# A new static order, tables partly on ScalarE, and a half-column transform for one batch, in a fused attention and Fourier-mixing kernel

## The chip, the cores and the metric

The kernel runs on one core of one Trainium2 chip. The metric is the device time of one execution in microseconds (us), as the median over several runs. A core has five engines with instruction queues of their own: PE (TensorE, the matrix engine), DVE (VectorE), ACT (ScalarE), POOL (GpSimd) and SP (SyncE, which here only issues DMA transfers). Matmuls write to PSUM, which has eight banks of 128 partitions by 512 fp32 numbers; everything else lies in SBUF.

## The reference

Four inputs r, k, v and w of shape (4 batches, 8 heads, 768 steps, 48) go through a linear attention with a decaying state; its output, 768 rows of 384 numbers per batch, is mixed by the real part of a two-dimensional Fourier transform, added to itself, normalised and passed through a two-layer perceptron.

```python
# attention, per batch and head; state is 48 x 48
for t in range(S):
    cur = outer(u * k[t], v[t])
    y[t] = r[t] @ (state + cur)
    state = w[t][:, None] * state + outer(k[t], v[t])
# x = y with the heads side by side: (4, 768, 384)
X = np.fft.fft(x, axis=1)                  # over the 768 steps
X = np.fft.fft(X, axis=2)                  # over the 384 columns
u  = x + np.real(X)
mu = mean(u, -1); var = mean((u - mu) ** 2, -1)
un = (u - mu) / sqrt(var + 1e-6)
out = u + np.maximum(un @ w_ch1, 0.0) @ w_ch2      # 384 -> 1536 -> 384
```

## The kernel before

**Chunks.** The 768 steps of each batch are cut in six chunks of 128, named (b,c) below. `attention(b, c)` takes the logarithm of w (ACT, into `LB`), sums it along the steps with two matmuls against masks (lines 773 and 777), takes exponentials, scales r and k (`RH`, `KH`), transposes them (matmuls against an identity in the first 18 chunks, a transposing DMA later, line 819), forms the scores (line 843: 48 rows of the array at a time), masks them (line 848), updates the state (lines 866 to 885; the state matmul is line 869) and forms y (lines 896 and 899) into `X`. `fold` adds and subtracts mirrored columns of `X`, so that the transform over columns needs half the work.

**Mix.** `mix(b)` does the transform over the 768 steps (line 968) into `HCS` and, mirrored by the symmetry of the result, `HCR`; then, for each of six row blocks kb, the transform over columns: three matmuls of 384 columns against the tables `DTM` (line 992), which add up in one PSUM bank. VectorE adds x to the bank (line 997) into `UF` and sums the row; ScalarE or VectorE centres it into `UN`; ScalarE sums the squares. `UN` is transposed (matmuls of line 1027 in the first two batches, a transposing DMA per half batch in the last two, line 1033) into `UNT`. Per half batch come the twelve W1 groups of three matmuls (line 1056), the ReLU into `HT` (line 1062 on VectorE, line 1064 on ScalarE), and three W2 blocks, each of three groups of four matmuls (line 1075), followed by the last scaling and addition (line 1081) and the store (line 1085).

**Tables.** The cosines and sines `CS` and `SS` are made on the chip at the start: integer steps and roundings (`TQ`, `TG`, `TF`) and two sine operations on ScalarE, then mirrored copies, then `DTM` by matmuls against the identity `IDW`. The zero paddings of several buffers are filled at the start, too. TensorE begins with sixteen matmuls (line 1098) on a filled piece of the weight buffer `W1`, and 36 filler matmuls (line 1130) stand in its list.

**Order.** Nothing is scheduled at run time. Every operation is a call of `op`, with one or several engines that may execute it and a planned duration for each. `ORDER`, five lists of operation numbers, says which engine executes what, and in which order. `schedule` replays the lists with the planned durations, chooses PSUM banks and adds a few waits between VectorE and POOL; `emit` then writes each engine's list with the semaphore waits that the data need. So a planned duration has no direct effect on the chip; the lists have. SP's list holds the 96 loads (192 KB each, seven buffers per input), the transposing DMAs and the stores; the three weight loads are issued by POOL: two halves of W1 (line 745) and W2 (line 749).

Of the kernel before, what the change touches and what calls it, by code (L numbers as in the profile page):

```python
# [7 lines left out]
ALU = mybir.AluOpType  # L8
# [27 lines left out]

MEANS = (0, 1, 2, 3)
# [29 lines left out]
    "act": (  # L67
# [14 lines left out]
    "dve": (  # L82
# [14 lines left out]
    "pool": (  # L97
# [12 lines left out]
}  # L110


class _Tile:


    __slots__ = ("bank", "ops", "pool", "n_done", "end")
# [1047 lines left out]
```

## Time and profile before

| | |
|---|---|
| median of 3 runs | 182.72 us (182.53 to 183.22) |
| the profiled execution | 184.21 us, of which the span from first to last instruction is 182.4 us |
| granted TensorE clock | 1.000 |
| busy share of the span | PE 97%, DVE 81%, ACT 71%, POOL 56% |
| HBM | 23.59 MB read, 4.72 MB written, 155 GB/s over the span |
| instructions | 4568, of them 1722 matmuls |

The profile shows one execution. For each engine it gives busy time and idle time, and for idle time what ended it. Rows of a group read: line, engine, operation, what it writes and reads, count, then busy time in us and the mean duration of one in ns, then the idle time before. Matmuls overlap, so the mean duration of one is longer than the distance from one to the next.

### The profile page before, as it was taken

Reading aid. Unit: us, or ns where it says so; the run is one execution under the profiler, and the core shown is the slowest. Engines: PE = TensorE matmul, PEld = TensorE weight load, DVE = VectorE, ACT = ScalarE, POOL = GpSimd, SP = SyncE. Lnnn points to the kernel's source line nnn. Section 1 sums busy time; section 2 is a strip of 40 time slices with the busy share of each in tenths; the row PEclk is TensorE's granted clock in tenths of the full one; section 3 lists DMA queues with packets and bytes.
Section 4 is the critical chain, followed back from the end, with each engine's and each line's share of the span. In section 5 each row is a group of like instructions: output and inputs, shape, how many; then the busy total and the mean of one; then the engine's idle time right before and its main releaser. Section 6 shows DMA issues by size and latency. Waiting matters only on the chain.

```text
span 182.4 us, 4568 instructions
## 1 busy us (share of the span) xinstructions
PE 176.8 (97%) x1722; PEld 116.3 (64%) x1722; DVE 148.2 (81%) x341; ACT 130.2 (71%) x340; POOL 101.5 (56%) x120
## 2 busy tenths in 40 slices
PE   7999999999999999999999999999999999999994
PEld 3465676766566666776657666656666676666663
DVE  8779999899899999999888997899979927622343
ACT  2889859597898675799899978888882247478200
POOL 2448789767231498589998968769653440000000
DMA  4999998999999899999999999997550103331214
GB/s 97 203 216 196 208 191 172 185 202 208 152 196 190 162 210 230 226 204 182 202 222 218 219 177 207 220 212 179 103 114 0 47 2 65 73 125 43 86 71 145
DMA packets 116119, 28.99 MB, mean 159 GB/s; under 512 B 111361, under 2 KB 116098, under 8 KB 116098
## 3 DMA queue, kind: packets, MB, share of 16 engines
q1 hardware_dynamic: 114514, 26.36, 70.2%
q0 software_dynamic: 1584, 2.36, 8.0%
q8 instruction: 13, 0.21, 0.5%
q14 instruction: 8, 0.07, 0.1%
HBM read 23.59 MB, written 4.72 MB: 155 GB/s over the span
## 4 chain that ended last, share of the span: by engine, by line
PE 61%; DVE 17%; DMA 9%; SPq 4%; ACT 4%; issue 3%; DVEq 0%
PE bank L1075 18%; PE bank L1056 17%; DMA in_w<-in_w_dram 5%; DMA w<-in_moe_w_ch_dram 4%; DVE ah L848 4%; SPq L609 4%; PE bank L992 3%; PE bank L1130 3%; PE bank L1098 3%; PE bank L968 3%; DVE osb L1081 2%; PE bank L843 2%; DVE rkh L561 2%; PE bank L889 2%; PE bank L899 2%
## 5 line engine op out<-in xcount | busy, mean ns | idle before, releaser
L1075 PE MATMUL bank<-w,ht 128*128 128x384 bf16 (+2 forms) x300 | 53.7, 320 | 0.0
L1056 PE MATMUL bank<-unt,w 128*128 128x384 bf16 x288 | 51.9, 326 | 0.6 <-DMA w<-in_moe_w_ch_dram 0.6
L1064 ACT ACTIVATE ht<-bank 128x384 bf16<-128x384 f32 x72 | 32.6, 496 | 9.3 <-PE bank L1056 8.9
L1056 PEld LDWEIGHTS bank<-unt,w 128*128 128x128 bf16 x288 | 26.9, 98 | 17.5 <-DVE ht L1062 0.8
L1075 PEld LDWEIGHTS bank<-w,ht 128*128 128x128 bf16 x300 | 27.5, 98 | 15.2
L848 DVE TENSOR_TENSOR ah<-bank,msk 128x512 bf16<-128x512 f32 x48 | 31.2, 682 | 2.1 <-PE bank L843 2.0
L561 POOL TENSOR_TENSOR rk<-rk,ub 128x384 f32<-128x384 f32 x21 | 21.6, 1034 | 8.6 <-DVE rk L561 7.0
L561 POOL TENSOR_TENSOR vtd<-in_v,dc 128x384 f32<-128x384 f32 x20 | 16.7, 837 | 11.2 <-DVE dc L800 8.1
L1081 DVE SCALAR_TENSOR_TENSOR osb<-bank,rstd,uf 128x384 f32<-128x384 f32 (+2 forms) x25 | 14.8, 596 | 9.5 <-PE bank L1075 5.9
L1062 DVE TENSOR_SCALAR ht<-bank 128x384 bf16<-128x384 f32 x24 | 13.0, 549 | 6.9 <-PE bank L1056 6.8
L561 POOL TENSOR_TENSOR rk<-in_r,in_k 128x384 f32<-128x384 f32 x17 | 16.9, 999 | 2.9 <-DMA in_r<-in_r_dram 1.4
L997 DVE SCALAR_TENSOR_TENSOR uf<-bank,x 128x384 f32<-128x384 f32 x24 | 12.5, 553 | 4.7 <-PE bank L992 4.6
L561 POOL TENSOR_TENSOR rkh<-in_k,e 128x384 bf16<-128x384 f32 x14 | 14.1, 1009 | 3.6 <-ACT e L792 2.0
L779 ACT ACTIVATE bank<-bank 128x384 f32<-128x384 f32 x24 | 11.5, 484 | 5.8 <-PE bank L773 5.8
L811 DVE TENSOR_TENSOR rkh<-bank,in_r 128x384 bf16<-128x384 f32 x24 | 13.1, 549 | 2.1 <-ACT bank L779 2.0
L575 ACT ACTIVATE xf<-uf,agg 128x384 bf16<-128x384 f32 x24 | 14.7, 614 | 0.0
L561 POOL TENSOR_TENSOR xf<-sd 128x382 bf16<-128x382 f32 (+1 forms) x10 | 10.6, 1062 | 6.5 <-DVE sd L561 3.0
L575 ACT ACTIVATE lb<-in_w 128x384 bf16<-128x384 f32 x24 | 12.4, 519 | 2.1 <-DMA in_w<-in_w_dram 1.8
L575 ACT ACTIVATE un<-uf,agg 128x384 bf16<-128x384 f32 x18 | 10.6, 611 | 4.1 <-DVE uf L997 4.1
L586 ACT ACTIVATE rkt<-bank 128x256 f32<-128x256 f32 x29 | 10.8, 389 | 3.6 <-PE bank L833 2.4
L561 POOL TENSOR_TENSOR sd<-x 128x385 f32<-128x385 f32 x10 | 10.0, 1015 | 5.9 <-DVE x L908 5.4
L792 ACT ACTIVATE e<-bank 128x392 f32<-128x392 f32 (+1 forms) x24 | 11.7, 497 | 2.3 <-DVE bank L877 1.0
(138 smaller groups left out, 358.7 us busy)
## 6 DMA issues: line engine op xcount, KB each, us to landing
in_w<-in_w_dram SPq DMA_DIRECT2D x24, 192.0 KB, 3.8
in_k<-in_k_dram SPq DMA_DIRECT2D x24, 192.0 KB, 3.8
in_r<-in_r_dram SPq DMA_DIRECT2D x24, 192.0 KB, 4.1
in_v<-in_v_dram SPq DMA_DIRECT2D x24, 192.0 KB, 4.0
out_dram<-osb SPq DMA_DIRECT2D x23, 192.0 KB, 2.8
w<-in_moe_w_ch_dram POOLq DMA_DIRECT2D x2, 576.0 KB, 8.1
w<-in_moe_w_ch_dram POOLq DMA_DIRECT2D x1, 1152.0 KB, 10.7
out_dram<-osb SPq DMA_DIRECT2D x1, 128.0 KB, 1.7
```

Of the source, the lines that this page charges most:

```text
L561: return lambda e: e.tensor_tensor(out=o, in0=a, in1=b, op=f)
L575: return lambda e: e.activation(o, a, f, **kw)
L779: op("act", a_ps(DM) + 20, lambda e: e.activation(ps(tce)[:, 0:DM], ps(tce)[:, 0:DM], ACTF.Exp), w=[tce])
L792: op("act", a_ps(ne), lambda e: e.activation(E2[i2][:, 0:ne], ps(tci)[:, 0:ne], ACTF.Exp), r=[tci], w=[("E2", i2)])
L811: op("dve", v_1(DM), lambda e: e.tensor_tensor(out=rh[:, :, 0:D], in0=ps(tce)[:, 0:DM].rearrange("t (h d) -> t h d", d=D), in1=rt[:, :, :] ...
L848: masked[n] = op("dve", v_1(512), lambda e, x=x: e.tensor_tensor(out=ah[:, x:H:2, :], in0=ps(ta[x])[:, :].rearrange("p (h t) -> p h t", t= ...
L997: op("dve", v_1(DM) + 60, lambda e, kb=kb, t=t: e.scalar_tensor_tensor(out=uf[:, kb, :], in0=ps(t)[:, 0:DM], scalar=1.0, in1=xb[:, kb, 0:D ...
L1056: ins = e.matmul(ps(t)[:, 0:384], W1[:, m, 256 * (j // 2) + j % 2:256 * (j // 2) + 256:2], unt[:, :, m, :], start=(m == 0), stop=(m == NM ...
L1062: {"dve": lambda e, j=j, t=t, ht=ht: e.tensor_scalar(out=ht[:, j, :], in0=ps(t)[:, 0:384], scalar1=su, scalar2=0.0, op0=ALU.mult, op1=ALU. ...
L1064: "act": lambda e, j=j, t=t, ht=ht: e.activation(ht[:, j, :], ps(t)[:, 0:384], ACTF.Relu, scale=su)},
L1075: ins = e.matmul(ps(t)[:, 0:hi - lo], ht[:, j, 128 * x:128 * x + 128], W2[:, j, lo:hi], start=(j == 0), stop=(j == NJ - 1))
L1081: op("dve", v_1(hi - lo) + 64, lambda e, kb=kb, t=t, o=o, lo=lo, hi=hi: e.scalar_tensor_tensor(out=o[:, lo:hi], in0=ps(t)[:, 0:hi - lo], s ...
```

## The change

Seven things change together.

1. In the planner a load takes 920 ns for batch 0 and 1030 ns for the others (960 before), an eviction of `HCS` on ScalarE and the folds on POOL are planned longer, and an operation can be marked as a fence behind the one before it on its engine (the two loads of ScalarE's tables of functions are).
2. Two of the three roundings `TQ`, the zero fills and the mirrored copies may now run on ScalarE; the new order puts two roundings and several fills there.
3. The identity `IDW` is made by VectorE in `NIDW` and copied by ScalarE, as pairs of 16-bit numbers.
4. For batch 3 (`HALF_OUT`) the transform over columns is done in half columns: columns k and 384 - k share a part A and differ in the sign of a part B, so A and B are formed for 193 columns each, and A + B and A - B give all 384. Per row block that is four matmuls of 193 columns, a copy of B by ScalarE, an add and a subtract by VectorE, and the addition of x with the row's sum.
5. Four small operations make the tables for this: `CQ` and the products `DTC`, `DTS` (kept where `CN` and `SN` were).
6. All five lists of `ORDER` are new. 37 operations move from ScalarE to VectorE and 35 the other way, 30 from POOL to VectorE and 28 the other way, 4 from ScalarE to POOL and 2 back. There are 24 operations more.
7. The order of loads, stores and weight loads on SP and POOL is new as part of this.

```diff
+HALF_OUT = (3,)
 ORDER = {
-    "pe": ("7 1414 68 1415 1416 ..."),
+    "pe": ("8 1438 1439 1440 1441 72 ..."),
...
+                if o.fence:
+                    o.deps.add(d)
...
-                if o.xfer == 960:
+                if o.xfer in (920, 1030):
...
-               w=[("in", n, i)], sem="in_%s%d" % (n, i), xfer=960)
+               w=[("in", n, i)], sem="in_%s%d" % (n, i), xfer=920 if b == 0 else 1030)
...
-        dset(384, ts(IDW[:, :], CI[:, :], 0.0, None, ALU.is_equal), r=["CI"], w=["IDB"])
+        dset(384, ts(NIDW[:, :], CI[:, :], 0.0, None, ALU.is_equal), r=["CI"], w=["NIDW"])
+        op("act", a_sb(192), lambda e: e.activation(IDW[:, :].bitcast(FP32), NIDW[:, :].bitcast(FP32), ACTF.Copy),
+           r=["NIDW"], w=["IDB"])
...
+    def zero(o, n, d, x, w):
+        src = TC[:, 0:1].unsqueeze(2).to_broadcast([128, o.shape[1], o.shape[2]])
+        op(None, {"dve": d, "pool": x, "act": a_sb(n)},
+           {"dve": fill(o, 0.0), "pool": fill(o, 0.0), "act": act(o, src, ACTF.Copy, scale=0.0)}, r=["TC"], w=w)
...
-            op(None, {"dve": 266, "pool": 520}, ts(TQ[:, q, :], KI[:, :], TN[:, q:q + 1], MAGIC, ALU.mult, ALU.add),
-               port=("dve",), r=["KI", "TN"], w=[("TQ", q)])
+            f = ts(TQ[:, q, :], KI[:, :], TN[:, q:q + 1], MAGIC, ALU.mult, ALU.add)
+            op(None, {"dve": 266, "pool": 520, "act": a_sb(2 * HQ) + 30},
+               {"dve": f, "pool": f, "act": act(TQ[:, q, :], KI[:, :], ACTF.Identity, scale=TN[:, q:q + 1], bias=MGC[:, :])},
+               port=("dve",), r=["KI", "TN", "MGC"], w=[("TQ", q)])
...
+        if b in HALF_OUT[:1]:
+            for z, T in enumerate((DTC, DTS)):
+                op(None, {"act": a_sb(HE), "dve": v_2(HE)},
+                   {"act": lambda e, z=z, T=T: e.activation(T, DTM[:, 1, 0:HE], ACTF.Copy, scale=CQ[:, z:z + 1]),
+                    "dve": ts(T, DTM[:, 1, 0:HE], CQ[:, z:z + 1], None, ALU.mult)}, port=("dve",),
+                   r=["DTM1", "CQ%d" % z], w=["DTH%d" % z, ("CSn", "SSn")[z]])
...
+            if b in HALF_OUT:
+                t = g.tile("f")
+                for j in (0, 2, 1):
+                    def f(e, j=j, kb=kb, t=t):
+                        a = 128 * (kb % NP)
+                        x = (hcs if kb < NP else HCR)[:, j, a:a + 128]
+                        if j != 1:
+                            return e.matmul(ps(t)[:, (HE if j else 0):(2 * HE if j else HE)], x, DTM[:, j, 0:HE], start=(j == 0),
+                                            stop=False, skip_group_check=True)
+                        e.matmul(ps(t)[:, 0:HE], x, DTC, start=False, stop=True, skip_group_check=True)
+                        return e.matmul(ps(t)[:, HE:2 * HE], x, DTS, start=False, stop=True, skip_group_check=True)
+                    op("pe", mm(HE, 2 if j == 1 else 1), f, ...)
...
+                if b in HALF_OUT:
+                    fs = SD[:, kb % 2, 0, 0:HE]
+                    op("act", a_ps(HE), lambda e, t=t, fs=fs: e.activation(fs, ps(t)[:, HE:2 * HE], ACTF.Copy),
+                       r=[t], w=[("SD", kb % 2, 0)])
+                    op("dve", v_1(HE), lambda e, kb=kb, t=t, fs=fs: e.tensor_tensor(
+                        out=uf[:, kb, 0:HE], in0=ps(t)[:, 0:HE], in1=fs, op=ALU.add), ...)
+                    op("dve", v_1(HE), lambda e, kb=kb, t=t, fs=fs: e.tensor_tensor(
+                        out=uf[:, kb, DM - 1:HE - 1:-1], in0=ps(t)[:, 1:HE - 1], in1=fs[:, 1:HE - 1], op=ALU.subtract), ...)
```

More of the change, by code (lines that the diff above doesn't have):

```diff
@@ L184, in op @@
         o.tiled = tiled
+        o.fence = fence
         for x in r:
@@ L218, in schedule @@
                 o.dur, o.fn, o.port = o.alts[e]
+            for d, o in zip(self.order[e], self.order[e][1:]):
+                if o.fence:
+                    o.deps.add(d)
         for o in self.ops:
@@ L509, in bass_rwkv6_finch__then__fnet_fourier_mix_kernel @@
     DTM = sb("dtm", [3, DM], BF16)
+    CQ = sb("cq", [2], FP32)
     IDW = sb("idw", [384], BF16)
@@ L519, in bass_rwkv6_finch__then__fnet_fourier_mix_kernel @@
     BHPI = sb("bhpi", [1], FP32)
+    MGC = sb("mgc", [1], FP32)
     TCI = sb("tci", [1], mybir.dt.int32)
@@ L579, in vec, with vecx @@
         return op(None, {"pool": p_1(n), "dve": v_1(n)}, fn, port=("dve",), **kw)
+    def vecx(n, fn, **kw):
+        return op(None, {"pool": p_1(n) + 80, "dve": v_1(n)}, fn, port=("dve",), **kw)
     def evict(o, i, n, x=1, more=0, **kw):
@@ L590, in dset @@
         return op("dve", v_2(n), fn, port=("dve",), **kw)
+    MAGIC = 12582912.0
     loads, asked = {}, {}
@@ L627, in small_constants @@
         op("dve", 30, fill(BHPI[:, :], PI / 2), w=["BHPI"])
+        op("dve", 30, fill(MGC[:, :], MAGIC), w=["MGC"])
     def masks():
@@ L647, in bonus, with flip @@
         o = evict(lambda: UB[:, :, :].rearrange("p h d -> p (h d)"), lambda: ps(t)[:, 0:DM], DM, r=[t, "LOGEXP"], w=["UB"])
-    def either(d, x, fn, **kw):
-        return op(None, {"pool": x, "dve": d}, fn, port=("dve",), **kw)
+    def flip(o, i, sg, **kw):
+        f = ts(o, i, sg, None, ALU.mult)
+        return op(None, {"pool": 740, "dve": 260, "act": a_sb(3 * HQ)},
+                  {"pool": f, "dve": f, "act": act(o, i, ACTF.Copy, scale=sg)}, port=("dve",), **kw)
+    def zero(o, n, d, x, w):
+        src = TC[:, 0:1].unsqueeze(2).to_broadcast([128, o.shape[1], o.shape[2]])
+        op(None, {"dve": d, "pool": x, "act": a_sb(n)},
+           {"dve": fill(o, 0.0), "pool": fill(o, 0.0), "act": act(o, src, ACTF.Copy, scale=0.0)}, r=["TC"], w=w)
     def fills():
@@ L656, in fills @@
                 if (n, i) != ("LB", 0):
-                    op(None, {"dve": 75, "pool": 150}, fill(T[i][:, :, D:64], 0.0), w=[(n, i)])
+                    zero(T[i][:, :, D:64], H * (64 - D), 75, 150, [(n, i)])
         for i in range(2):
             for lo, hi, n, z in ((0, 64, "XFn", "XFz"), (446, 512, "XFo", "XFz2")):
-                op(None, {"pool": 250, "dve": 180}, fill(XF[i][:, :, lo:hi], 0.0),
-                   w=[(z, i)] + [(n, i, c) for c in range(NC)])
-            op(None, {"pool": 100, "dve": 60}, fill(X[i][:, :, DM:DM + 4], 0.0), w=[("X", i, c) for c in range(NC)])
-    MAGIC = 12582912.0
+                zero(XF[i][:, :, lo:hi], NC * (hi - lo), 180, 250, [(z, i)] + [(n, i, c) for c in range(NC)])
+            zero(X[i][:, :, DM:DM + 4], NC * 4, 60, 100, [("X", i, c) for c in range(NC)])
     def tables():
@@ L718, in tables_end @@
                r=[(n, q) for q in range(NP)], w=[n + "n"])
-        small(150, ts(NIDW[:, :], IDW[:, :], -1.0, None, ALU.mult), r=["IDB"], w=["NIDW"])
+        op(None, {"dve": 160, "act": a_sb(384)}, {"dve": ts(NIDW[:, :], IDW[:, :], -1.0, None, ALU.mult),
+                                                  "act": act(NIDW[:, :], IDW[:, :], ACTF.Copy, scale=-1.0)},
+           port=("dve",), r=["IDB"], w=["NIDW"])
         small(62, ts(CP[:, :], TC[:, 0:1], 62.5, None, ALU.is_gt), r=["TC"], w=["CP0"])
-        small(62, ts(CP[:, :], CP[:, :], 2.0, -1.0, ALU.mult, ALU.add), r=["CP0"], w=["CP"])
+        small(62, ts(CQ[:, 1:2], CP[:, :], -1.0, 1.0, ALU.mult, ALU.add), r=["CP0"], w=["CQ1"])
+        small(62, ts(CQ[:, 0:1], CP[:, :], 1.0, None, ALU.mult), r=["CP0"], w=["CQ0"])
+        small(62, ts(CP[:, :], CP[:, :], 2.0, -1.0, ALU.mult, ALU.add), r=["CP0"], w=["CP", "CP0"])
         moves = ([(True, 0, 0, 128, -64), (True, 1, 0, 128, 64)],
@@ L919, in fold @@
         if b < FOLD:
-            vec(192, tt(xf[:, c, 64:256], xb[:, c, 0:192], xb[:, c, 384:192:-1], ALU.add),
+            vecx(192, tt(xf[:, c, 64:256], xb[:, c, 0:192], xb[:, c, 384:192:-1], ALU.add),
                 r=[("X", i, c)], w=[("XFe", i, c)])
-            vec(191, tt(xf[:, c, 256:447], xb[:, c, 1:192], xb[:, c, 383:192:-1], ALU.subtract),
+            vecx(191, tt(xf[:, c, 256:447], xb[:, c, 1:192], xb[:, c, 383:192:-1], ALU.subtract),
                 r=[("X", i, c)], w=[("XFo", i, c)])
@@ L936, in fold @@
         have = [("SD", z, 0), ("SD", z, 1)]
-        vec(DM, tt(xf[:, p:NC:NP, 64:256], sd[:, :, 0:192], sd[:, :, 384:192:-1], ALU.add),
+        vecx(DM, tt(xf[:, p:NC:NP, 64:256], sd[:, :, 0:192], sd[:, :, 384:192:-1], ALU.add),
             r=have, w=[("XFe", i, p), ("XFe", i, c)])
-        vec(DM, tt(xf[:, p:NC:NP, 256:447], sd[:, :, 1:192], sd[:, :, 383:192:-1], ALU.subtract),
+        vecx(DM, tt(xf[:, p:NC:NP, 256:447], sd[:, :, 1:192], sd[:, :, 383:192:-1], ALU.subtract),
             r=have, w=[("XFo", i, p), ("XFo", i, c)])
@@ L973, in mix @@
             evict(lambda j=j: hcs[:, j, :].rearrange("p (n x) -> p x n", x=2),
-                  lambda t=t: ps(t)[:, 0:2 * HE].rearrange("p (x n) -> p x n", x=2), 2 * HE, r=[t], w=[("HCS", j)], more=85)
+                  lambda t=t: ps(t)[:, 0:2 * HE].rearrange("p (x n) -> p x n", x=2), 2 * HE, r=[t], w=[("HCS", j)], more=125)
             sg = (1.0, CP[:, :], -1.0)[j]
@@ L987, in mix, with f @@
             n = b * NC + kb
-            t = g.tile("f")
-            for j in range(3):
-                def f(e, j=j, kb=kb, t=t):
-                    a = 128 * (kb % NP)
-                    return e.matmul(ps(t)[:, 0:DM], (hcs if kb < NP else HCR)[:, j, a:a + 128], DTM[:, j, :], start=(j == 0), stop=(j == 2))
-                op("pe", mm(DM), f, r=[("HCS" if kb < NP else "HCR", j), "DTM%d" % j], w=[t])
+            if b in HALF_OUT:
[9 more added lines that the diff above has]
+                        return e.matmul(ps(t)[:, HE:2 * HE], x, DTS, start=False, stop=True, skip_group_check=True)
+                    op("pe", mm(HE, 2 if j == 1 else 1), f, r=[("HCS" if kb < NP else "HCR", j), "DTM%d" % j]
+                       + (["DTH0", "DTH1"] if j == 1 else []), w=[t])
+            else:
+                t = g.tile("f")
+                for j in range(3):
+                    def f(e, j=j, kb=kb, t=t):
+                        a = 128 * (kb % NP)
+                        return e.matmul(ps(t)[:, 0:DM], (hcs if kb < NP else HCR)[:, j, a:a + 128], DTM[:, j, :], start=(j == 0), stop=(j == 2))
+                    op("pe", mm(DM), f, r=[("HCS" if kb < NP else "HCR", j), "DTM%d" % j], w=[t])
             iu = (2 * b + kb // 3) % len(UN)
@@ L996, in mix @@
             if b in MEANS:
-                op("dve", v_1(DM) + 60, lambda e, kb=kb, t=t: e.scalar_tensor_tensor(
-                    out=uf[:, kb, :], in0=ps(t)[:, 0:DM], scalar=1.0, in1=xb[:, kb, 0:DM], op0=ALU.mult, op1=ALU.add,
-                    accum_out=agg[:, kb, 0:1]), r=[t, ("X", i, kb)], w=[("UF", i, kb), ("SUM", i, kb)])
+                if b in HALF_OUT:
[3 more added lines that the diff above has]
+                    op("dve", v_1(HE), lambda e, kb=kb, t=t, fs=fs: e.tensor_tensor(
+                        out=uf[:, kb, 0:HE], in0=ps(t)[:, 0:HE], in1=fs, op=ALU.add),
+                       r=[t, ("SD", kb % 2, 0)], w=[("UFa", i, kb), ("UF", i, kb)])
+                    op("dve", v_1(HE), lambda e, kb=kb, t=t, fs=fs: e.tensor_tensor(
+                        out=uf[:, kb, DM - 1:HE - 1:-1], in0=ps(t)[:, 1:HE - 1], in1=fs[:, 1:HE - 1], op=ALU.subtract),
+                       r=[t, ("SD", kb % 2, 0)], w=[("UFb", i, kb), ("UF", i, kb)])
+                op("dve", v_1(DM) + (60 if b in HALF_OUT else 10), lambda e, kb=kb, t=t: e.scalar_tensor_tensor(
+                    out=uf[:, kb, :], in0=uf[:, kb, :] if b in HALF_OUT else ps(t)[:, 0:DM], scalar=1.0, in1=xb[:, kb, 0:DM],
+                    op0=ALU.mult, op1=ALU.add, accum_out=agg[:, kb, 0:1]),
+                    port=("dve",) if b in HALF_OUT else (),
+                    r=[("UFa", i, kb), ("UFb", i, kb), ("X", i, kb)] if b in HALF_OUT else [t, ("X", i, kb)],
+                    w=[("UF", i, kb), ("SUM", i, kb)])
                 op(None, {"act": a_sb(DM) + 95, "dve": v_2(DM) + 60},
```

13 lines of the change are left out of this document (6 added, 7 removed), and 129 rows, old and new, of the table ORDER.

## The prediction

> **What bounds the kernel now.** I read the page's parts 1 and 2 first, then the chain of waits in order of time, then what TensorE waited for.
>
> ```profile
> span 182.4 us, 4568 instructions
> PE 176.8 (97%) x1722; PEld 116.3 (64%) x1722; DVE 148.2 (81%) x341; ACT 130.2 (71%) x340; POOL 101.5 (56%) x120
> ```
>
> A busy PE need not be a PE at its peak, so 97% alone proves little. The chain settles it (start, length, what):
>
> ```profile
> 1.31 5.30 PE bank L1098 x16
> ...
> 146.27 0.84 PE bank L968 x10
> ...
> 152.00 0.97 PE bank L992 x6
> ...
> 153.78 2.60 PE bank L1075 x16
> 156.38 7.80 PE bank L1056 x48
> ...
> 179.92 0.35 DVE osb L1081
> ```
>
> Divide length by count. 7.80/48 is 162.5 ns for 384 columns, in 2.60/16 and 0.97/6 the same; 0.84/10 is 84 ns for 193 columns. From about 152 to 180 us TensorE issues one matmul after the other at the rate of its columns; the last VectorE piece only closes the chain. The sixteen opening matmuls take 5.30/16, twice that, whatever they compute. Now its real waits (line, what for, us, times, longest):
>
> ```profile
> PE bank L1098 <- DVE w L572: 1.3, 1, 1.3
> PE bank L1056 <- DMA w<-in_moe_w_ch_dram: 0.6, 1, 0.6
> PE bank L777 <- ACT ht L1064: 0.3, 1, 0.3
> PE bank L833 <- POOL rkh L561: 0.3, 1, 0.3
> ```
>
> Behind the start, little is waited for. TensorE executes a fixed list, so the end is its start, plus its matmuls, plus the stalls; one saved stall counts only until the next thing is late. Adding up the matmuls of the list at these rates, I find about 2 us of stall after the start-up: an estimate from those rates and the end of the last matmul.
>
> The profiled execution took 184.21 us, 1.8 us more than its span of 182.4; the median of the runs is 182.72, 1.5 us under it. I work out differences on the span and carry them to the median unchanged. A difference under 0.5% (0.91 us) is about what measuring this kernel cannot tell from none.
>
> **Half columns.** In batch 3 each of six row blocks had three matmuls of 384 columns and now has four of 193. Removed: 18 x 162.5 ns = 2.93 us. Added: 24 x 84 ns = 2.02 us. TensorE saves 0.91 us, and these matmuls are on the chain. In the row the ten matmuls at 84 ns each have a weight load of their own. The Trainium skill (TensorE: Matmul & The Clock Gate, sections LDWEIGHTS and Back-to-back issue gap) gives a load as its columns over 1.2, 107 ns for 128 columns, and says that load and matmul together set the spacing; were the load the limit, 24 would cost an estimated 2.57 us and the saving shrink to 0.36. The 84 ns disagree. I keep 0.91.
>
> What each block gains elsewhere: a ScalarE copy of 193 columns, a VectorE add and a subtract, and the old full-width operation. Nearest rows, and the transpose that follows:
>
> ```profile
> L586 ACT ACTIVATE unt<-bank 128x192 f32<-128x192 f32 x12 | 3.5, 330 | 0.4 <-PE bank L1027 0.4
> L569 DVE SCALAR_TENSOR_TENSOR uf<-osb,tc,ht 128x194 f32<-128x194 f32 x3 | 1.1, 411 | 0.0
> L997 DVE SCALAR_TENSOR_TENSOR uf<-bank,x 128x384 f32<-128x384 f32 x24 | 12.5, 553 | 4.7 <-PE bank L992 4.6
> L566 DVE TENSOR_SCALAR un<-uf,agg 128x384 bf16<-128x384 f32 x6 | 2.8, 499 | 0.1
> unt<-un SPq DMA_TRANSPOSE x4, 3.3
> ```
>
> VectorE gains 12 x 0.37 (1.1/3) = 4.4 us, ScalarE 6 x 0.33 = 2.0. Both lie beside TensorE's work as long as the first transposed half is there in time. Cover, from block 0's last matmul to batch 3's first W1 matmul in the new list: 15 half matmuls (1.26), one W1 group (3 x 162.5 = 0.49), eleven W2 groups of four (11 x 0.65 = 7.15): 8.9 us. Chain: copy 0.33; eight half operations, three full and one normalisation on VectorE, 8 x 0.37 + 3 x 0.55 + 0.47 = 5.1; transpose 3.3; three hand-overs of 0.1. Sum 9.0 when nothing overlaps, late by 0.1; where the in-order operations overlap by 0.1 each, 8.0. I take nothing, with 0.1 as upper end, and less than nothing is excluded, since no earlier transposed half can move a TensorE list that has no gap there. For the second half nine more W1 groups and one W2 group (5.0) are cover. Of the reversed copies two go from ScalarE to POOL; their first readers stand some twenty matmuls behind the ones that fill them, so I cost that at nothing too.
>
> **The scores' neighbours.** These use 48 rows:
>
> ```profile
> 136.22 0.65 PE L1056 MATMUL bank<-unt,w 128*128 128x384 bf16 x3
> 136.81 0.62 PE L843 MATMUL bank<-rkt 48*128 48x128 bf16 x16
> 137.36 0.50 PE L1075 MATMUL bank<-w,ht 128*128 128x384 bf16 x2
> ```
>
> Three matmuls from 136.22 are issued by 136.71, yet the scores begin at 136.81: 0.1 us to go over, and as much back. The old list goes over 18 times, the new one 17. Saved: 0.2.
>
> **Start.** The weight fill that the opening matmuls wait for was VectorE's first instruction; a zero fill of 0.27 us and two tiny ones now stand ahead.
>
> ```profile
> 0.87 0.38 DVE L572 MEMSET w<- 128x384 bf16 x1 [0.87 <-PEq L1149]
> 1.42 0.27 DVE L572 MEMSET lb<- 128x256 uint32 x1
> ```
>
> All of TensorE starts about 0.3 us later; the number of filler matmuls stays 36, so nothing gives this back: +0.3 (0 to 0.4). Table steps on ScalarE fall into its idle time before the sines.
>
> **W1.** The one DMA wait above, 0.6 us, is for the second half of W1. POOL issues it like this (start, length):
>
> ```profile
> 35.63 0.50 POOL L982 COPY hcr<-hcs 128x384 bf16<-128x384 bf16 x1 [1.09 <-ACT hcs L586]
> 36.10 1.00 POOL L561 TENSOR_TENSOR rkh<-in_k,e 128x384 bf16<-128x384 f32 x1
> 37.82 0.80 POOL L745 DMA_DIRECT2D w<-in_moe_w_ch_dram  x1 [0.73 <-DVE rkh L561]
> 45.93 0.88 POOL L749 DMA_DIRECT2D w<-in_moe_w_ch_dram  x1
> ```
>
> In the new order it stands ahead of that copy and product, 1.5 us of POOL work, and its first reader stands at the same point of TensorE's list. The wait goes: -0.6 (-0.6 to 0).
>
> **Loads.** SP's list is permuted too. Batch 0's pace, and w of chunk (0,4), whose logarithm the matmul at 17.84 needs:
>
> ```profile
> DMA packets 11117, 2.10 MB, mean 210 GB/s; under 512 B 11117, under 2 KB 11117, under 8 KB 11117
> L609 SPq DMA_DIRECT2D in_w<-in_w_dram x1: 867/867/867, 10.7 to 10.7; - x1
> DMA to landing us min/median/max: 3.7/3.7/3.7
> 17.84 0.32 PE L777 MATMUL bank<-lb,nle 128*128 128x384 bf16 x1
> L575 ACT ACTIVATE lb<-in_w 128x384 bf16<-128x384 f32 x24 | 12.4, 519 | 2.1 <-DMA in_w<-in_w_dram 1.8 <-POOL lb L572 0.2
> ```
>
> 196.6 KB at 210 GB/s is 0.94 us a load. This one landed at 14.4 and is now three loads later: 17.2. The logarithm (0.52) and two hand-overs of about 0.1 make it 17.9, and its matmul, moved little, comes at 17.7 to 18.0. So 3.4 us of slack become none, and v of that chunk loses about as much. Between 0 and 1.5; I take +0.4, nearer to the lower end, because this row sits on the edge and not behind it.
>
> **Moves.** 37 operations go from ScalarE to VectorE and 35 back, 30 from POOL to VectorE and 28 back: apart from batch 3's end each engine keeps its sum. The load lengths, and the dearer evictions and folds, are only numbers of the planner: nothing by themselves.
>
> Sum: -0.91 - 0.2 + 0.3 - 0.6 + 0.4 = -1.0. 182.72 - 1.0 = **181.7 us**.
>
> **Rivals.**
>
> *Early loads eat it* (same). If (0,4)'s loads cost the upper 1.5 instead of 0.4, the sum is +0.1: 182.8. For: the slack gone. Against: fillers stand around these matmuls.
>
> *Weight loads pace the half matmuls* (same).
>
> ```profile
> L968 PEld LDWEIGHTS bank<-cs,xf 128*128 128x128 bf16 x42 | 3.6, 97 | 1.0
> ```
>
> At 97 ns each, 24 cost 2.33, saving 0.60 and not 0.91: 182.0. This is the skill's issue-gap rule in this trace's numbers; the 84 ns speak against it.
>
> *W2 holds back batch 1* (slower). While W2 moves, loads issued after it hang. The v of chunk (1,2):
>
> ```profile
> L609 SPq DMA_DIRECT2D in_v<-in_v_dram x1: 706/706/706, 46.3 to 46.3; - x1
> DMA to landing us min/median/max: 10.7/10.7/10.7
> 60.52 0.33 PE L869 MATMUL bank<-vb,rkh 128*128 128x96 bf16 x4
> L575 ACT ACTIVATE vb<-in_v 128x384 bf16<-128x384 f32 x22 | 11.5, 528 | 0.5 <-DMA in_v<-in_v_dram 0.5
> ```
>
> W2 was issued at 45.93; this load landed at 57.0 and was used at 60.52. In the new list its state matmul stands 4.7 us of TensorE work earlier, at 55.8, and the load is one place later. If it still hangs it lands at 57.0 or, at 0.94 behind, 57.9; with its cast and a hand-over (0.53 + 0.1) TensorE waits 1.8 to 2.7 us; w of (1,5) stands just ahead of it in the list. Sum -1.0 + 2.7 = +1.7: 184.4. It decides as soon as this load is issued after W2 and the wait passes 1.9 us. Against: W2 now stands behind POOL work on k of the same chunk, loaded five places earlier, so the stream may get through first.
>
> *The reordering does nothing* (same): W1 waits as before, TensorE goes over as often, and only the half columns and the later start remain, -0.6: 182.1. Against: both list positions are plain in the diff.
>
> **Numbers.** Forecast 0.46; early loads 0.17; weight loads 0.06; half columns only 0.07; W2 0.21; 0.01 for other gains, 0.02 for other losses. So faster 0.46 + 0.01 = 0.47, same 0.17 + 0.06 + 0.07 = 0.30, slower 0.21 + 0.02 = 0.23. The forecast sits close to the line of 0.5% (181.81). Low end: the other stalls of the waits' rows (0.3 + 0.3) and a start that costs nothing (0.3) and loads that cost nothing (0.4), 181.7 - 1.3 = 180.4. High end: into the W2 case (183.5 to 184.4), 183.9, which leaves out its worse half. The forecast's own range is 180.4 to 182.6.
>
> **What would show it.** Right: the batch 3 matmuls at 84 ns in the chain; no wait of L1056 on the weights; the opening matmuls starting near 1.6; W1 groups of batch 3 following the W2 groups without a gap. Wrong: matmuls at 97 ns or over; TensorE waiting before the first W1 group of batch 3; gaps on TensorE at 17 to 30 us for loads of (0,4), or at 55 to 58 us with in_v or in_w landing over 10 us after their issue. A gain above 1.9 us would mean that I took stalls for granted which the order sets.

## The result: 0.9% slower, and the profile after

The changed kernel takes 184.58 us (median of 20 runs, 182.54 to 186.31), the kernel before beside it 182.69 (20 runs, 181.54 to 183.51). The ratio is 1.0092, with a 95% interval of 1.0069 to 1.0115. A gain of 1.0 us was forecast; it became a loss of 1.7, or 1.9 between the medians. (A median is over all executions; the ratios leave out those more than 1.5% above the fastest of the same kernel, three of the changed kernel's twenty here and six of twelve in e13, so the two can differ.)

The two profiles shown, before's in the prediction and after's here, have the same span of 182.4 us, but before's is of an execution 1.5 us above its median, and after's (184.48 us) of one at its median. Two further profiles of the kernel before (183.18 and 181.87 us) are used below.

The page of the changed kernel, its head, and what TensorE waited for (line, what for, us, times, longest):

```profile
span 182.4 us, 4603 instructions
PE 175.7 (96%) x1728; PEld 116.2 (64%) x1728; DVE 152.8 (84%) x361; ACT 130.5 (72%) x344; POOL 101.4 (56%) x120
...
PE bank L1158 <- DVE w L581: 1.6, 1, 1.6
PE bank L869 <- DMA rkt<-rkh: 1.1, 1, 1.1
PE bank L869 <- DVE x L934: 0.7, 1, 0.7
PE bank L922 <- DVE ht L1122: 0.2, 1, 0.2
```

L1158 are the opening matmuls. Before, the next row was the wait for W1; that one is gone. New are two waits of the scores (L869; L843 in the code before) and one of y (L922). All three lie in batch 3's attention, where before had no single stall over 0.4 us. The chain of waits in order of time (start, length, what) shows how they come about:

```profile
1.64 5.03 PE bank L1158 x16
...
33.69 11.10 DMA in_k<-in_k_dram
...
99.72 0.39 ACT e L818
100.11 0.10 ACT rstd L1106
100.21 0.06 issue
100.27 1.19 POOL rkh L570
101.46 0.03 POOL rk L570
101.49 4.95 DMA rkt<-rkh
106.44 0.14 issue
...
128.66 1.24 SPq L845
129.90 0.04 issue
129.95 4.39 DMA in_v<-in_v_dram
134.34 0.02 issue
134.36 0.98 DVE vb L834
135.34 0.48 DVE x L934
135.82 0.05 issue
135.87 0.40 PE bank L869 x8
...
146.18 0.50 PE bank L1028 x6
...
157.90 8.78 PE bank L1116 x54
```

First: POOL finishes the scaled k of chunk (3,0) at 101.46, SyncE at once issues its transposing DMA (L845), and that takes 4.95 us. TensorE was ready 1.3 us before the scores could start at 106.58. Second: SyncE's list is in order, and v of (3,4) stands behind the transposing DMA issued at 128.66, which itself waited for VectorE's scaled r (128.03 to 128.60). So the load is issued at 129.95 and lands at 134.34. VectorE's cast waits for it, the addition that frees a PSUM bank (L934) waits behind the cast, and the scores of (3,5) wait for that bank until 135.87. Third, and shorter: VectorE idles 0.71 us for r of (3,5) before 129.30, the ReLU of L1122 comes later by it, and y waits for that until 130.85.

Between two matmuls one can count what their distance exceeds the columns of the first (162.5 ns per 384, at least 64 columns; fp32 matmuls at their own distance, the sixteen opening ones at 320 ns). Summed over stretches, us (e11, below, is the changed kernel with three moves in batch 3):

| | before: 184.21 / 183.18 / 181.87 us | after: 184.48 us | e11: 181.73 us |
|---|---|---|---|
| start of the first matmul | 1.31 / 1.31 / 1.31 | 1.64 | 1.64 |
| to 30 us | 1.79 / 0.70 / 1.21 | 1.91 | 2.01 |
| 30 to 50 | 0.82 / 0.30 / 0.16 | 0.71 | 0.47 |
| 50 to 105 | 0.86 / 1.57 / 0.15 | -0.27 | -0.32 |
| 105 to 137 | 0.37 / 0.14 / -0.13 | 1.85 | -0.35 |
| 137 to the end | -0.03 / 0.07 / 0.06 | 0.30 | 0.19 |

(Short matmuls in pairs go faster than their 64 columns, hence the negative ones. Stalls in the expectations below are counted at 160 ns per 384 columns and so come out larger, by the same amount for every kernel.) Against the third execution of before the sum for after is 3.38 higher; less 0.91 for the half columns that is 2.5, and the spans differ by 182.4 - 180.0 = 2.4. For e11 it is 0.88 - 0.91 = 0.0, and the spans are 179.9 and 180.0.

The row to 30 us needs care. The opening matmuls stand 320 ns apart up to some moment and 163 from then on, and this moment differs by execution: all sixteen took 5.30, 4.43 and 5.06 us in the three executions of before, 5.03 in after and 5.30 in e11. So 0.9 of the 1.1 us between before's first two executions in this row is the opening, and both had the same order.

### The profile page after: what moved, and what is told of

It is laid out like the page before. It is cut to its first block, busy times and chain, and to the rows that moved or that the text cites. A ratio compares the mean times of both kernels' runs of the same rounds, so it can differ in the third digit from the quotient of the medians.

```text
span 182.4 us, 4603 instructions
## 1 busy us (share of the span) xinstructions
PE 175.7 (96%) x1728; PEld 116.2 (64%) x1728; DVE 152.8 (84%) x361; ACT 130.5 (72%) x344; POOL 101.4 (56%) x120
## 4 chain that ended last, share of the span: by engine, by line
PE 73%; DMA 11%; DVE 6%; SPq 4%; POOL 2%; issue 1%; ACT 1%; DVEq 0%
PE bank L1135 24%; PE bank L1116 17%; DMA in_k<-in_k_dram 6%; PE bank L1001 3%; PE bank L1039 3%; PE bank L869 3%; SPq L623 3%; PE bank L1158 3%; DMA rkt<-rkh 3%; DMA in_v<-in_v_dram 2%; PE bank L853 2%; PE bank L925 2%; PE bank L1190 2%; PE bank L915 2%; PE bank L922 2%; PE bank L799 2%
## 5 line engine op out<-in xcount | busy, mean ns | idle before, releaser
L1116 PE MATMUL bank<-unt,w 128*128 128x384 bf16 x288 | 53.6, 326 | 0.0
L1135 PE MATMUL bank<-w,ht 128*128 128x384 bf16 (+2 forms) x300 | 52.9, 320 | 0.0
L1116 PEld LDWEIGHTS bank<-unt,w 128*128 128x128 bf16 x288 | 26.7, 98 | 16.1 <-DVE ah L874 0.3
L570 POOL TENSOR_TENSOR rk<-rk,ub 128x384 f32<-128x384 f32 x22 | 22.8, 1042 | 4.8 <-DVE rk L570 2.5
L570 POOL TENSOR_TENSOR rkh<-in_k,e 128x384 bf16<-128x384 f32 x16 | 16.2, 1014 | 12.4 <-DMA in_k<-in_k_dram 6.0
L570 POOL TENSOR_TENSOR rk<-in_r,in_k 128x384 f32<-128x384 f32 x19 | 19.4, 1026 | 4.3 <-DVE cq L574 1.7
L1122 DVE TENSOR_SCALAR ht<-bank 128x384 bf16<-128x384 f32 x26 | 14.0, 551 | 7.1 <-PE bank L1116 7.1
L570 POOL TENSOR_TENSOR vtd<-in_v,dc 128x384 f32<-128x384 f32 x19 | 15.8, 839 | 1.6 <-DVE dc L826 1.4
L826 DVE TENSOR_REDUCE dc<-rk 128x8 f32<-128x384 f32 x24 | 12.9, 545 | 0.8 <-POOL rk L570 0.8
L584 ACT ACTIVATE vb<-in_v 128x384 bf16<-128x384 f32 x20 | 10.6, 532 | 1.3 <-DMA in_v<-in_v_dram 1.2
L570 POOL TENSOR_TENSOR xf<-sd 128x382 bf16<-128x382 f32 (+1 forms) x8 | 7.9, 1000 | 6.3 <-ACT ht L1124 2.5
```

The costliest lines, as they stand in the source:

```text
L570: return lambda e: e.tensor_tensor(out=o, in0=a, in1=b, op=f)
L584: return lambda e: e.activation(o, a, f, **kw)
L826: op("dve", v_1(DM), lambda e: e.tensor_reduce(out=dc[:, :], in_=rku[:, :, :], axis=mybir.AxisListType.X, op=ALU.add), r=[("RK", i2)], w=[ ...
L1116: ins = e.matmul(ps(t)[:, 0:384], W1[:, m, 256 * (j // 2) + j % 2:256 * (j // 2) + 256:2], unt[:, :, m, :], start=(m == 0), stop=(m == NM ...
L1122: {"dve": lambda e, j=j, t=t, ht=ht: e.tensor_scalar(out=ht[:, j, :], in0=ps(t)[:, 0:384], scalar1=su, scalar2=0.0, op0=ALU.mult, op1=ALU. ...
L1135: ins = e.matmul(ps(t)[:, 0:hi - lo], ht[:, j, 128 * x:128 * x + 128], W2[:, j, lo:hi], start=(j == 0), stop=(j == NJ - 1))
```

## The experiments

The theory was that late waits in batch 3, made by the new lists, cost what was lost. Rivals: the half columns cost; the front costs; or the waits only trade places. A moved entry is not quite alone: `schedule` then also picks other banks for some operations (268 of 1474 in e1 and e11, none in e5 and e9). Ratios are to the kernel before in the same comparison, with 95% intervals. Diffs show the moved entry and its new neighbours.

**The kernel before again, twice (e0, e10).**

> The kernel before, once more, for a second profile of it, since the first one is of an execution 1.5 us above its median. All theories: 182 to 183 us, with a span near 181. Late-waits theory (the new order leaves two or three long waits of TensorE in batch 3's attention): a fast execution of before has no single stall of TensorE over 0.8 us after 50 us. Front theory (what was lost, was lost before 60 us): the stalls of before in its first 60 us sum to at least 1.5 us less than those of the changed kernel.

> The kernel before a third time, for its spread between executions: the first two profiles are of 184.21 and 183.18 us. The front, up to 30 us, took 3.4 us of stalls with the start in the first and 2.3 in the second; a faster execution should have less still, and 50 to 105 us less than 1.7.

183.18 and 181.87 us. No single stall after 50 us exceeds 0.77 us in the first and 0.30 in the second: as the late-waits theory had it. But the front's expectation holds too, at least in e10. Start and stalls up to 50 us come to 2.31 and 2.68, against 4.26 in after; of the 1.95 between e0 and after, 0.6 is the opening (4.43 against 5.03 us), of the 1.58 between e10 and after nothing. The third profile's front is not the shortest of the three, its 50 to 105 us is.

**Scores of (3,0) later (e1).**

```diff
 PE: W2 group of batch 1
-    scores (3,0)
     scores (2,5); totals of (3,2); W2 group; W1 group
+    scores (3,0)
     sums of (3,1)
```

> The changed kernel with one entry of TensorE's list moved: the scores of chunk (3,0) stand one W2 group and one W1 group and a half later (1.5 us), behind the matmul for (3,1). Late-waits theory: the stall of 1.29 us at 106.6 us shrinks to under 0.3 and most of it stays won to the end, 184.6 - 1.0 = 183.6. Rival, the half columns cost: no change, 184.6. Rival, the front costs: no change, 184.6. Rival, given back later: the stall goes, but TensorE waits as much in batch 3's later scores: 184.6 with new stalls between 110 and 137 us.

183.49 us, 1.0066 (1.0028 to 1.0104). The wait for the transposing DMA is gone, those at the later scores are not:

```profile
PE bank L1158 <- DVE w L581: 1.6, 1, 1.6
PE bank L869 <- DVE x L934: 0.7, 1, 0.7
PE bank L853 <- DVE rkh L837: 0.6, 2, 0.4
```

Nothing took its place later: 105 to 137 us falls from 1.85 to 0.81. The ratio falls by 0.0026 (0.5 us), which is inside the intervals; e6, with two moves more, falls by 0.0047, outside of them.

**Two loads earlier (e2), and both (e3).**

```diff
 SP: load (3,5).k
+    load (3,5).r; load (3,4).v
     transposing DMA (3,2); (3,3); store; UNT of batch 2, first half; ...
-    load (3,5).r ... transposing DMA (3,4); load (3,4).v
```

> The changed kernel with two loads moved in SyncE's list: r of (3,5) and v of (3,4) go ahead of the transposing DMA of (3,2), and so land about 8 us earlier. Late-waits theory: VectorE no longer idles for them at 129 and 134 us, the stalls of 0.40 at 130.9 and 0.84 at 135.9 go: 184.6 - 1.2 = 183.4. Rivals, half columns or front: 184.6. If transposing DMAs suffer from loads behind them: those of (3,2) and (3,3) get over 4 us and scores there wait, 184.6 to 185.5.

> Both moves together. Late-waits theory: the gains add, 184.6 - 2.2 = 182.4, at or under the kernel before. Rivals, half columns or front: 184.6. Given back later: between 183.4 and 184.6.

184.36 us, 1.0111 (1.0057 to 1.0165), and 184.63, 1.0139 (1.0079 to 1.0198). The two late loads hold up nothing any more (and in e3 the scores of (3,0) don't wait either), but a wait of 0.8 came, for batch 2's transposed half, which the two loads push back on SyncE; e2's row:

```profile
PE bank L1116 <- DMA unt<-un: 0.8, 1, 0.8
```

So what was won was given back at another transposing DMA. In e3's profile the front was hit as well (waits of TensorE, and the rows of engines, granted clock, DMA share and GB/s by stretch):

```profile
PE bank L803 <- ACT lb L584: 1.8, 1, 1.8
...
16.00:18.00 2.00, 2.00 (x20) 1.32 (x20) 2.00 (x5) 0.81 (x3) 1.73 (x2) 1.00 1.13 222
18.00:20.00 2.00, 0.17 (x7) 0.06 (x3) 0.79 (x2) 0.57 (x2) 0.12 (x1) 1.00 0.39 74
20.00:22.00 2.00, 2.00 (x30) 1.46 (x30) 1.12 (x3) 2.00 (x7) 1.92 (x3) 1.00 1.01 198
```

From 18 to 20 us the transfers nearly paused (74 GB/s), w of (0,4) took 5.9 us, and TensorE waited for its logarithm. This is the case that the prediction priced at up to 1.5.

**The front's parts (e4, e5, e6).** w of (0,4) two places earlier; the weight fill first on VectorE; and both with e1's move.

```diff
 SP:  load (0,2).r
+     load (0,4).w
      load (0,5).w; load (0,3).k
 DVE:
+     weight fill W1x
      MGC; BEPS; zero fill LB0
```

> The changed kernel with one load moved in SyncE's list: w of chunk (0,4) goes two places earlier, ahead of w of (0,5) and k of (0,3), and so is issued near 11 us instead of 13 to 13.5. Early-loads theory (in the executions in which the DMA engines pause near 18 to 20 us, TensorE waits up to 2 us for this load): the slow end of the times goes, the median falls by 0.3 to 1.0, 183.6 to 184.3, and no stall of TensorE at the first matmul of (0,4). Rival, the pause of the DMA engines holds back another load just as long: 184.6, with a stall of TensorE at another chunk's matmul between 18 and 30 us. Half columns or batch 3's waits as sole causes: 184.6.

> The changed kernel with the weight fill moved back to the head of VectorE's list, ahead of the zero fill. Later-start theory: the opening matmuls start near 1.3 instead of 1.64 us and the whole follows, 184.6 - 0.3 = 184.3. Rival, the early loads set the front: TensorE starts 0.3 us earlier and waits 0.3 us more before 25 us, 184.6.

> The changed kernel with three moves: scores of (3,0) later on TensorE (1.1 us won when it was done alone), w of (0,4) two places earlier on SyncE, the weight fill first on VectorE. If the three costs are separate: 184.6 - 1.1 - 0.5 - 0.3 = 182.7, level with the kernel before. If the front is set by loads whatever their order: 183.5.

184.48 us, 1.0104 (1.0050 to 1.0158); 184.13, 1.0106 (1.0058 to 1.0153); 182.85, 1.0045 (1.0013 to 1.0078). Neither of the first two shows a gain. In e5 TensorE starts 0.33 us earlier and then waits for the first logarithm; the rival held, with a logarithm as what is late and not a load:

```profile
PE bank L1158 <- DVE w L581: 1.3, 1, 1.3
PE bank L803 <- ACT lb L584: 0.9, 1, 0.9
```

Only about 0.3 of this wait comes from the earlier start. In e5's execution the opening matmuls took 4.39 us, 0.64 less than in after; in e6, with the same start and 5.13 us, TensorE stalls 0.30 us before the same matmul.

**Loads ahead of the transposing DMA of (3,0) (e9).**

```diff
 SP: load (3,1).k
+    load (3,4).w; load (3,3).v; load (3,2).v
     transposing DMA (3,0)
```

> The changed kernel with w of (3,4), v of (3,3) and v of (3,2) moved in SyncE's list from behind to ahead of the transposing DMA of (3,0), into time in which SyncE waits for that DMA's data. If the loads issued behind it make the transposing DMA long: it lands 3.2 to 3.6 us after its issue instead of 4.95, and the stall of TensorE at 106.6 us falls from 1.3 to about 0. If any loads in flight do, ahead or behind: 4.5 to 5 us, and the stall stays. If waiting for data sets it: issue stays at 101.5 either way.

It is issued at 101.6 as before and lands after 5.3 us; that it can't be issued sooner is POOL's doing. The scores wait 1.9 us, and 186.38 us is the time, more than this wait explains (see the last section).

The 5.3 us is what the second case named, but loads in flight are not shown to be the cause. The changed kernel's transposing DMA of 110.2 us took 3.1 with five loads in flight, and one of e2, issued at 129.8, took 4.8 with none. What goes with the long ones is another transfer. From 101.5 to 106.4 us in after, the rows of the DMA queues (packets, MB, share) are

```profile
q1 hardware_dynamic: 2020, 0.45, 86.9%
q8 instruction: 1, 0.02, 1.2%
```

and from 110.2 to 113.3 the second row is missing. In the nineteen profiles there are 114 transposing DMAs of scaled r and k. 35 took 4.6 to 5.3 us, and each of them had such a packet of 16 KB, kind instruction, starting 1.4 to 3.0 us behind its issue; of the 79 that took 3.1 to 4.4 us only one had (3.1 us, in e0). No run moved these packets, so that they are the cause is not shown either. Loads can add something: the second `UNT` transposing DMA of batch 2 took 3.8 us in after and 4.0 to 4.5 with r of (3,5) ahead of it (e11, e8).

**Five moves (e8), and the late waits alone (e11).** The loads go into gaps in which SyncE waits anyway; e11 has these and e1's move and nothing else.

```diff
 SP: UNT of batch 2, first half; store
+    load (3,5).r
     UNT of batch 2, second half; load (3,5).v; store
+    load (3,4).v
     transposing DMA (3,4)
```

> The changed kernel with five moves: the three of the run before (scores of (3,0) later, w of (0,4) two places earlier, the weight fill first; 182.85 us, 1.0045 of the kernel before) and two loads in SyncE's list: v of (3,4) goes ahead of the transposing DMA of (3,4), r of (3,5) ahead of the second transposing DMA of batch 2's mix, both into time in which SyncE waits for those transposes' data. Late-waits theory: the stalls of 0.40 at 130.8 and 0.84 at 135.8 us go and no transposing DMA is issued later, 182.85 - 1.2 = 181.6, level with or faster than the kernel before. Rival, given back to a transposing DMA as when r of (3,5) and v of (3,4) were both put ahead of (3,2)'s: a new stall of 0.9 us before batch 2's W1 groups or at the scores, 182.5 to 182.9.

> The changed kernel with its front untouched and only the three moves against batch 3's late waits: scores of (3,0) later on TensorE, v of (3,4) ahead of the transposing DMA of (3,4), r of (3,5) ahead of batch 2's second transposing DMA. Late-waits theory: the stalls of 1.3, 0.4 and 0.84 us go, 184.6 - 2.2 = 182.4 (1.001 to 1.003 of the kernel before). If a good part of the gain with five moves came from the front's two moves: 183 to 183.5 (1.005).

182.33 us, 1.0019 (0.9991 to 1.0048), and 182.41, 1.0018 (0.9987 to 1.0049). The front's two moves show no gain (0.3 us would be hidden in the intervals); three moves in batch 3 take the loss back, to level with before. The 1.0 us that was forecast they do not bring: in the table, start and stalls up to 50 us are still 4.12 in e11, against 3.92, 2.31 and 2.68 in before. By stretch, in the third profile of before, in after and in e11 (the first entry after the length is TensorE's busy time):

```profile
105.00:137.00 32.00, 31.89 (x304) 20.42 (x303) 28.90 (x63) 25.89 (x68) 23.02 (x25) 1.00 0.81 154
```
```profile
105.00:137.00 32.00, 29.96 (x306) 19.51 (x305) 28.97 (x63) 24.82 (x62) 20.38 (x22) 1.00 0.91 176
```
```profile
105.00:137.00 32.00, 32.00 (x334) 21.11 (x333) 30.41 (x67) 25.50 (x64) 21.59 (x24) 1.00 0.91 175
```

2.0 us of idle TensorE in after, none in e11. By the ratios the moves are worth 1.0092 - 1.0018 = 0.0074 (0.0035 to 0.0113: 0.6 to 2.1 us), by the table 2.2.

**k of (1,2) ahead of W1 (e12).** On e8, one load three places earlier:

```diff
 SP: load (1,0).k
+    load (1,2).k
     load (1,3).w; load (1,2).r; load (1,0).v
```

> The kernel with five moves (1.0019 of the kernel before) and a sixth: k of (1,2) goes three places earlier in SyncE's list, so that it is issued near 31 us and not at 34.1, right behind the weight load W1's first half of 34.12. Theory that weight loads hold it back: it lands near 35 to 36 instead of 45.4, POOL no longer waits 6.2 us for it, the stall of 0.42 us before the transposes of (1,2) near 49.8 us goes, and the time falls by 0.2 to 0.5: 0.997 to 1.001 of before. Rival, another load takes its place behind the weights (k of (1,0) or w of (1,3), moved later by it): a new stall of its size, 1.002.

182.32 us, 1.0018 (0.9985 to 1.0051). k lands 3.7 us after its issue and POOL no longer waits, but v of (1,0) is now the one behind the weights (11.3 us), and through ScalarE a W1 group of batch 0 waits:

```profile
PE bank L1116 <- ACT unt L598: 0.6, 1, 0.6
...
ACT vb L584 <- DMA in_v<-in_v_dram: 0.6, 1, 0.6
```

The rival held, though the load that took the place is another than it named.

**The front of the kernel before (e13), with e12's move (e14).** All start-up, table and batch 0 operations with their loads as before, merged by time into e8's lists.

```diff
 SP:
-    u; (0,2).w; (0,0).w; (0,1).w; (0,0).k; (0,0).r; (0,0).v; (0,1).r; ...
+    (0,1).w; u; (0,0).w; (0,0).k; (0,0).r; (0,1).k; (0,0).v; (0,1).r; ...
 (PE, DVE, ACT, POOL alike)
```

> The kernel with five moves, and its front put back: all operations of the start-up, of the tables and of batch 0's attention, with their loads, on the engines and in the order of the kernel before (the identity made in one step as before), merged by time with the rest of the changed lists. Front theory: the stalls up to 30 us, with the start, fall from 4.0 us to 2.3 to 2.8 as in the kernel before, 1.2 us less, and the time to 0.995 to 0.996 of before. Rival, they are the price of the later part's earlier work (same stalls later): no change, 1.002.

> The two together: the front of the kernel before and k of (1,2) ahead of the weight load. If both are separate costs: 0.992 to 0.994 of before, 180.7 to 181.2 us. If either only moves a wait: 0.996 to 1.002.

185.31 us, 1.0061 (1.0012 to 1.0111), and 184.81, 1.0084 (1.0044 to 1.0124): slower, by 1.7% and 1.4% between the medians. The merge failed at its seam. Batch 0's loads as before push back w of (1,2), for which the changed TensorE list asks at 26 us; in e14 it landed at 28.35, and

```profile
PE bank L803 <- ACT lb L584: 2.5, 1, 2.5
```

Start and stalls up to 25 us, ahead of the seam, were 3.4 and 2.6 us, against 2.2 to 3.3 in before and 3.2 to 3.9 in eleven profiles with the changed front (5.5 in e3). The opening matmuls took 5.30 us in e13 and 4.61 in e14. Where they are slow, the fronts are close: 3.3 in before's first profile, 3.4 in e11. Where they are fast, the changed front gives it back in a wait for the first logarithm (0.5 us in e8, 0.9 in e5, 1.0 in e12), and before's front has no such row (e0, e14). That leans to the front theory, for some executions, and does not settle it.

**Tables back on VectorE (e15), and whole columns (e7, e16).** e15 is e11 with two roundings `TQ` on VectorE, table steps ahead of fills. e7 is the changed kernel, e16 is e15, with batch 3 in whole columns.

```diff
 DVE:
+     weight fill; MGC; identity; BHPI; TN; TQ1; TQ0; TQ2; TG; TF ...
      BEPS; zero fill LB0; ...
 ACT: TRIG
-     TQ0; TQ2
```
```diff
-HALF_OUT = (3,)
+HALF_OUT = ()
```

> The kernel with the three moves against batch 3's late waits (1.0018 of the kernel before), and the two roundings that the change put on ScalarE back on VectorE, directly behind the first fill, with the zero fills and masks behind the table steps. Theory that the longer chain of table steps holds the front (rounding on ScalarE until 3.1 us, sines from 4.8, the first logarithm from 7.8 and TensorE waiting for it): sines start near 4.4, the first logarithm near 7.4, and TensorE, starting 0.33 us earlier, has no wait over 0.4 us for it at 8.3: 0.3 to 0.4 us less, 0.9995 to 1.000. Rival, the loads of (0,0) and (0,1) and VectorE's own later masks set the front: no change, 1.002.

> The kernel of the run before this one with batch 3's transform in whole columns again, at the same lists. Half columns worth what was forecast, now that nothing late stands ahead of them: 0.9 us more than with half columns, 1.005 of the kernel before if that one is at 1.000. Rival, their operations on VectorE and ScalarE cost part of it back: 0.3 us more, 1.002.

> The changed kernel with batch 3's transform over columns in whole columns again: three matmuls of 384 columns per row block, no copy of the difference part, no half-width add and subtract, no DTC and DTS; all lists otherwise as changed. Half columns as predicted: 184.6 + 0.9 = 185.5. Rival, they gain nothing or cost because of their operations on VectorE and ScalarE: 184.6 or less; then a wait of TensorE before the first W1 group of batch 3 in the changed kernel would have to be gone here, and none was seen there.

e15: 182.30 us, 1.0002 (0.9969 to 1.0035). No wait for the first logarithm stands in its profile, but none stands in e11's either (opening 5.08 and 5.30 us). Up to 30 us TensorE stalls 2.34 where e11 had 2.01, so start and stalls are the same 3.65. e16 has e15's front and opened in 4.15 us; there TensorE waits for a mask, which now stands behind the table steps, as the rival had it:

```profile
PE bank L1190 <- DVE msk L574: 1.0, 1, 1.0
```

e16: 183.00, 1.0047 (1.0021 to 1.0073). e7: 184.65, 1.0133 (1.0083 to 1.0183), 0.0041 over the changed kernel's 1.0092, inside the intervals. Whole columns cost 0.0045 over e15 (0.8 us; the intervals together leave 0.1 to 1.6). The traces are sharper, with the last long row of W1 groups in the chain of e15 and of e16:

```profile
155.72 8.78 PE bank L1116 x54
```
```profile
156.78 8.78 PE bank L1116 x54
```

1.06 us later with whole columns, of which 0.16 is stall before 50 us.

No version here beats the kernel before: with the late waits out, the changed kernel is level with it. Half columns put into before's own lists were not tried: they need the work around batch 3's end rearranged.

## Why the prediction was wrong

*Half columns, -0.91: right.* The chain has six half matmuls in 0.50 us, 83 ns each, and e16 against e15 gives 1.06 - 0.16 = 0.9. No wait of L1116 stands before batch 3's first W1 group, so the 8.9 us of cover held. The Trainium skill (TensorE: Matmul & The Clock Gate, LDWEIGHTS and Back-to-back issue gap) gives a weight load as its columns over 1.2, an estimated 107 ns for 128 columns, and says that load and matmul together set the spacing. In this trace the loads of L1028 take 97 ns and the matmuls stand 83 apart, so the load does not set it here. That rival is out.

*Moves, "nothing by themselves": the step that failed.* I put the move of every operation and load behind 60 us at nothing, because each engine kept its sum, and took the waits there as given. But the positions moved against each other. The row that would have told it lay in the trace of before: the transposing DMA of (3,0) took as long there (issue at 104.5, time to landing),

```profile
DMA to landing us min/median/max: 5.0/5.0/5.0
...
110.88 0.40 PE L843 MATMUL bank<-rkt 48*128 48x128 bf16 x8
```

and the scores stood 1.4 us behind its landing. The new lists bring these scores forward by 5.6 us (110.88 to 105.3, where TensorE was ready), the DMA by 3.0 (104.5 to 101.5). Likewise I followed the loads of (0,4) and (1,2) to their readers, and none of batch 3's. These late waits cost 1.3 + 0.4 + 0.84 as single stalls, 2.2 in the table. They turn the forecast gain into a loss; that e11, without them, is level with before and not 1.0 us faster lies in the terms for W1 and the front below.

*Later start, +0.3: seen, but not a price.* The first matmul starts at 1.64 as forecast. Moved back (e5; e8 beside e11), it brings nothing that these runs can tell: in e6 the 0.33 us come back as 0.30 before the first logarithm, and start and stalls up to 30 us are 3.65 in e11 and in e15, which starts 0.33 earlier. "Nothing gives this back" was wrong.

*W1, -0.6: the wait is gone, the gain is not.* From 30 to 50 us the changed kernel stalls 0.71, between before's 0.16 and 0.82. The weights now hang ahead of k of (1,2) (11.10 us in the chain; POOL waits 6.0), and e12 shows that another load takes the place. This is the mechanism of the W2 rival, one weight half earlier and at 0.3 to 0.5 instead of 2.7; at 55 to 58 us, where that rival put it, there is no gap.

*Early loads, +0.4 (0 to 1.5): seen in one execution only.* In after w of (0,4) landed at 16.6 and not at 17.2, and its matmul waited for nothing, as in most profiles; in e3 it landed at 19.4 and TensorE stalled 2.0, more than my upper end. Start and stalls to 30 us are 3.55 in after and 2.0 to 3.1 in before, 0.4 to 1.5 more, but which part of the front is to blame stays open: e4, e5 and e15 each moved one and moved nothing, and e13 and e14 failed at their seam.

*Scores' neighbours, -0.2: not seen apart.* The stretch from 50 to 105 us has 0.4 to 1.8 us less than before's three profiles; this is a gain that I had not summed, mostly waits for loads and banks of batches 1 and 2 that before has and after has not.

By the table, against the mean of before's three profiles: front, start included, and 30 to 50 us, +1.3; 50 to 105, -1.1; late waits +1.7; end +0.3; half columns -0.9. Sum +1.2, where 184.48 less the mean of 183.09 gives 1.4.

## What to carry to other kernels

When a whole order is made anew, list every DMA that TensorE's next operation has waited behind or only just not, and compare how far its issue and its reader have each moved; equal sums per engine say nothing. On a queue that issues in order, look at what stands behind each blocking entry: a load there comes as late as that entry's data, and a better place is the time in which the queue waits anyway. A gain that the change does make, here 0.9 us, can be seen only once those waits are out.

## What the runs showed of the hardware

A long wait of TensorE cost more than itself. In e9 it stalled 2.1 us before 107.06, and then the granted clock (the entry behind the five engines) halved, by these rows for 3.4 us:

```profile
107.00:108.00 1.00, 0.94 (x23) 0.80 (x24) 0.28 (x1) 0.07 (x1) 1.00 (x2) 1.00 1.01 254
108.00:109.00 1.00, 1.00 (x5) 0.45 (x4) 1.00 (x3) 0.53 (x2) 0.52 (x1) 0.51 1.19 241
109.00:110.00 1.00, 1.00 (x4) 0.44 (x3) 0.61 (x2) 0.04 (x1) 0.00 (x0) 0.50 0.13 26
110.00:111.00 1.00, 1.00 (x17) 0.96 (x16) 0.40 (x1) 0.83 (x2) 0.00 (x0) 0.50 0.00 0
111.00:112.00 1.00, 1.00 (x10) 0.59 (x7) 1.00 (x3) 0.74 (x2) 0.00 (x0) 0.78 0.00 0
```

e14 did the same behind a stall of 2.6 us (2.5 in its row); e3, with 2.0 (1.8 in its row), did not. That 2.1 did and 2.0 did not is too little to say that the length alone decides. The Trainium skill (TensorE: Matmul & The Clock Gate, Part 1: The HAM clock gate) has the clock halve after at least one idle window of about 3.4 us; here 2.1 us were enough.

The transposing DMA of 128 x 1024 numbers took 3.1 to 4.4 us in 79 cases of 114 and 4.6 to 5.3 in the other 35, all of which had a 16 KB packet of kind instruction beside them (under e9); the number of loads in flight does not tell the two apart.

The opening matmuls, 384 columns each, took 4.15 us in one execution (e16) and 5.30 in others: they stand 320 ns apart at first and 163 later, while the granted clock in the rows is 1.00 in both stretches (e0, 1.3 to 4.7 and 4.8 to 5.6 us).
